# A searched instruction order: weights loaded first on one queue, token LayerNorm moved to GpSimd

## The chip, the cores and the metric

The kernel runs on one core of one Trainium2 chip. The metric is the device time of one execution in microseconds, as the median of several runs. The engines are TensorE (PE; its weight loads are shown apart as PEld), VectorE (DVE), ScalarE (ACT), GpSimd (POOL) and SyncE (SP), which issues transfers. All run side by side, each takes its own instructions strictly in the order in which they were written down, and they wait for one another by semaphores.

## The reference

Two layers; each is an attention block without a softmax over positions, and then a gated block. There are S = 2048 tokens (16 tiles of 128), D = 576 features, H = 32 heads of 18, and F = 4608 hidden features. All inputs are bf16.

```python
def A(x, wqkv, w_phi, wo):
    q, k, v = split(x @ wqkv)                       # 32 heads of 18
    pq, pk = q @ w_phi, k @ w_phi                   # per head
    phi_q = concat(softmax(pq), softmax(-pq))       # over 18 values: 36 features a head
    phi_k = concat(softmax(pk), softmax(-pk))
    kv = einsum("bhsf,bhsd->bhfd", phi_k, v)        # a sum over all tokens
    z  = phi_k.sum(over s)
    o = (phi_q @ kv) / (phi_q @ z + 1e-6)
    return o @ wo

def B(x, w_gate, w_up, w_down):
    return ((x @ w_gate) * (x @ w_up)) @ w_down

x = A_x
for layer in (1, 2):
    x = x + A(layernorm(x), wqkv, w_phi, wo)
    x = x + B(layernorm(x), w_gate, w_up, w_down)
```

`kv` needs every token's `phi_k` and `v` before the first output of the block can be made. So at the start of layer 1 all 16 token tiles go through layer norm, transposition, two projections and the softmax on the key side, and only then the gated block can begin. In the later part of a layer, the key side of the next layer is strewn into the gated block.

## The kernel before

The file does not write its instructions down in order. It describes them as some hundred small threads (generators), and a list scheduler, which runs when the kernel is built, picks the next operation again and again by an estimated time. The recorded order of each engine, with the semaphore waits it needs, is then emitted. Numbers in the code such as `Op(790, ...)` are those estimates in nanoseconds; they steer the order and are no measurements.

The choice of the next operation. `AGES` is a table of biases by thread name which was found by search, `th.age` a bias that a thread sets itself; `alt` offers one operation on several engines and takes the one that would end first:

```python
if r[0] == "alt":
    for i_, (eng, ops) in enumerate(r[1]):
        e_ = self.port_time(eng, ops[0], max(self.free_at[eng], self.ready(th, i_, eng, ops, False), th.t_ready))
        f_ = e_ + sum(o.dur for o in ops) * self.alt_cost[eng]
        if pick is None or f_ < pick[0]:
            pick = (f_, e_, eng, ops)
# ...
key = (est - self.bias.get(int(th.prio), 0.0) - th.age - th.age0 - (self.hold if late else th.boost), -th.prio)
# the smallest key is next
_, th, est = best
if self.fill is not None:
    self.keep_warm(min(pe_est, est))
```

`keep_warm` fills pauses of TensorE with products of a tile of zeros (L935), as many as the estimate says there is room for:

```python
def keep_warm(self, limit):
    t = self.free_at["pe"]
    # ...
    cold = 2.0 if t < 6000.0 else 1.0
    n = int((limit - (150.0 if early else 400.0) - t) / (56.0 * cold))
    for _ in range(n):
        o = self.fill(b, self.pe_mode)     # matmul of zt (128x128 zeros) with itself
        # ... recorded on TensorE if it ends before limit
```

The first loads. `x0` is one token tile (128 x 576, 147 KB), `x` two token tiles, `raw` one of five blocks of the query and key weights (128 x 1216, 311 KB), `wv` the value weights. `sload` is issued by SP, `aload` by ACT after the small `w_phi`:

```python
self.sload = [['x0', 0], ['raw', 0], ['x0', 1], ['raw', 2], ['raw', 3], ['raw', 4], ['wv', 0], ['x', 3]]
self.aload = [['raw', 1], ['x', 1], ['x', 2]]
```

A flag is then computed from the weights: it bounds how large `pq` and `pk` can become. All engines wait for it (L250, L251) and branch: if it is set, the *fast* program follows, in which the exponentials need no subtraction of a maximum; otherwise the *general* one. With these inputs the fast program runs. The flag takes ten products of each of the five weight blocks with themselves (L974), a norm of `w_phi` (L954 to L961), and two last products (L985):

```python
def t_flag(self):
    yield ("age", s.fage2)
    for kt in range(5):
        yield ("wait", ("ld", "raw", s.rord[kt]))
        # ten 128x128 products of Wraw[kt] with itself, into two banks        (L974)
    # two maxima on VectorE, compared with the limit                          (L977, L983)
    # one product with ones, then flag = (sum > 255.5)                        (L985, L987)
    yield ("mark", ("flag",))
    yield ("sig", "branch")
```

Query and key weights are multiplied with `w_phi` on the chip: each block is transposed by TensorE (L1100), evicted (L1103), multiplied with the block diagonal `BDphi` (L1114), and evicted to `Wq` or `Wk` (L1119).

Layer norm of one or two token tiles (`t_ln`). `fast` in this function is not the program but the variant with a TensorE transposition, which only urgent tiles use; the others are transposed by a DMA from `xln`, for which 640 columns are wanted, the last 64 being the last 64 of 576 once more:

```python
# statistics: two bn_stats per tile (L1154), bn_aggr (L1162), -mean (L1168 / L1171)
# rstd = exp(-0.5 * ln(var + eps)) on ScalarE                           (L1175, L1177)
em = [(lambda e, j=j, a=a, b=b, c=c: e.tensor_scalar(xln[:, sl[j], a:b], x_sb[:, ss[j], c:c + b - a],
            s.nmean[:, sl[j]:sl[j] + 1], rstd[:, sl[j]:sl[j] + 1], ALU.add, ALU.mult))
      for a, b, c in ((0, 576, 0), (576, 640, 512))[:2 - fast]]                       # L1187
yield ("alt", [(eng, [Op(d, em[i], ...) for i, d in enumerate(dur)])
               for eng, dur in (("pool", (790, 370)[:2 - fast]), ("dve", (400,) if fast else (400, 215)))[:1 + (fast or boot)]])
```

`boot` is true for the tiles at the start of layer 1. So there each tile's normalisation is one `tensor_scalar` over 576 columns and one over 64, on GpSimd or VectorE.

The key side of a tile: a projection into two banks (L1228, 18 products with 64 rows each, pairs of which share the array), four exponentials on ScalarE (L1349), then

```python
def softmax_tail(self, sm, crit, pz=None, exps=True):
    # sum over 18 values: tensor_reduce 128x1152 on VectorE                   (L1416)
    # 1/sum: reciprocal on VectorE (L1419), or Ln and Exp on ScalarE (L1423, L1427)
    for br in range(2):
        # dd = dd * (1/sum), 128x576, on GpSimd; on VectorE for the last two tiles  (L1431)
```

and 18 products for each pair of tiles that add to `kv` (L1470). The value projection is evicted by ScalarE (L1460). After the last pair: a mask (L1561), the numerator (L1618), a division (L1626 to L1640), the output projection (L1216), layer norm, transposition (L1195, L1198), and the gated block (L1758; downward products L1832 and L1834). Query projections are kept in `xT` and fill TensorE where they can.

Of the kernel before, what the change touches and what calls it, by code (L numbers as in the profile page):

```python
# [8 lines left out]
ALU = mybir.AluOpType  # L9
# [10 lines left out]
    "ain1_0": 96, "ain1_1": 52, "ain1_11": -60, "ain1_12": -492, "ain1_13": 86, "ain1_14": -147, "ain1_5": -137, "ain1_6": -193, "ain1_9": -273,  # L20
    "ain2_14": -438, "ain2_15": -340, "aout1_0": -130, "aout1_1": -102, "aout1_2": -169, "aout1_3": -149, "aout2_0": -365, "aout2_1": 28,
    "aout2_2": -170, "aout2_3": -392, "bar1": -205, "bar2": 31, "bdphi": 104, "bepi0": -915, "bepi6": 256, "bepi7": -330, "flag": -70, "fusek0": -120,
    "fusek1": -40, "fusek2": 301, "fusek3": -147, "fuseq0": -35, "fuseq1": -124, "fuseq2": -148, "fuseq3": -151, "init": 401, "k2_6": -418,
    "k2ln0": 766, "k2ln1": 1415, "kv2_7": -134, "lnA1_0a": 245, "lnA1_0b": 360, "lnA1_2": 62, "lnA1_3": 52, "lnA1_4": -54, "lnB1_0a": -675,
    "lnB1_0b": -631, "lnB2_0a": -815, "lnB2_0b": -579, "pq1_10": -131, "pq1_11": 213, "pq1_2": 262, "pq1_3": -196, "pq1_4": -111, "pq1_5": 12,
    "pq1_6": 145, "pq1_9": 334, "pq2_11": 118, "pq2_12": 428, "pq2_15": 112, "pq2_2": 322, "pq2_3": 281, "pq2_4": 41, "pq2_5": 296, "pq2_6": -35,
    "pq2_8": -91, "v1_0": 39, "v1_1": -420, "v1_11": -111, "v1_13": -244, "v1_15": 580, "v1_2": -281, "v1_3": -122, "v1_5": -127, "v1_6": -124,
    "v1_8": -122, "v2_14": -755, "v2_15": -878,
# [268 lines left out]
class Sched:  # L297

    def __init__(self, tracker):
# [13 lines left out]
        self.fill = None  # L313
        self.pe_switch = 100.0
# [94 lines left out]
    def keep_warm(self, limit):  # L409

        tr = self.tr
        t = self.free_at["pe"]
# [10 lines left out]
        b = max(cand)[1]  # L423
        cold = 2.0 if t < 6000.0 else 1.0
# [10 lines left out]
    def run(self):  # L435
        tr = self.tr
        while True:
# [122 lines left out]
            if r[0] == "ops":  # L560
                eng = r[1]
# [3 lines left out]
                for o in r[2]:  # L565
# [8 lines left out]
                    fin = t + o.dur  # L574
                    tr.record(eng, o.emit, o.reads, o.writes, o.excl, fin, deps)
# [7 lines left out]
            else:  # L583
# [7 lines left out]
                else:  # L591
                    start = max(issue + 1250.0, self.dma_free["sp"])
                    left, u = nbytes, start
                    for end, rate in ((3400.0, 290.0), (5000.0, 150.0), (1e9, 335.0)):
                        if u < end and left > 0:
                            d_ = min(left / rate, end - u)
                            left, u = left - d_ * rate, u + d_
# [3 lines left out]
                fin = max(start + xfer + (self.dma_lat if hasattr(self, "mark_time") else 600.0), issue + 2.1 * sp_time) + (1500.0 if sp_time > 1000 else 0.0)  # L601
# [66 lines left out]
class K:  # L668
    def __init__(self, nc, A_x, A_wqkv, A_w_phi, A_wo, B_w_gate, B_w_up, B_w_down, out, fast, base=None):
# [10 lines left out]
        self.vlead = 5  # L680
        self.row2 = True
        self.wtdma = ''
        self.valt = False
        self.qalt = True
        self.sload = [['x0', 0], ['raw', 0], ['x0', 1], ['raw', 2], ['raw', 3], ['raw', 4], ['wv', 0], ['x', 3]]
        self.aload = [['raw', 1], ['x', 1], ['x', 2]]
        self.rord = (0, 1, 2, 3, 4)
        self.fage = 300
        self.fageq = 0.0
        self.fage2 = 300  # L690
# [4 lines left out]
        self.qlead = 12 if fast else 8  # L695
# [8 lines left out]
        self.pqg = 8 if fast else 10  # L704
# [7 lines left out]
        self.fqp = 6.5 if fast else 6.5  # L712
# [225 lines left out]
    def t_bdphi(self):  # L938
        s = self
        yield ("wait", "init")  # L940
        yield ("wait", ("ld", "wphi5"))
        wb = s.wst5[:].unsqueeze(2).to_broadcast([128, 5, GH, DH])
# [5 lines left out]
    def t_m2(self):  # L948
# [3 lines left out]
        yield ("wait", ("ld", "wphi5"))  # L952
        yield ("age", s.fage2)
# [11 lines left out]
    def t_flag(self):  # L965
        s = self
        yield ("wait", "init")
        yield ("age", s.fage2)
        for kt in range(5):
            yield ("wait", ("ld", "raw", s.rord[kt]))  # L970
# [599 lines left out]
    def t_aout(self, L, st_):  # L1570
# [71 lines left out]
        if st_ >= 2:  # L1642
            ops.append(Op(130, (lambda e: e.tensor_copy(o[:, 576:640], o[:, 512:576])), reads=okeys, writes=okeys))
# [479 lines left out]
```

## Time and profile before

The median of three runs is 1074.42 us (1073.74 to 1075.68). The profiled execution has a span of 1073.7 us and a granted TensorE clock of 0.999.

| engine | busy, us | share | instructions |
|---|---|---|---|
| TensorE products | 1054.6 | 98% | 15797 |
| TensorE weight loads | 808.6 | 75% | 15859 |
| VectorE | 484.3 | 45% | 983 |
| ScalarE | 347.0 | 32% | 839 |
| GpSimd | 196.5 | 18% | 226 |

Points in time that the text comes back to, from the timeline:

| what | us |
|---|---|
| first load issued | 0.79 |
| first product of zeros | 1.03 |
| first product with weights (L974) | 5.45 |
| flag written (L987) | 17.93 to 18.06 |
| first key projection (L1228 with `Wk`) | 20.34 |
| first and last group of key-value products (L1470) | 33.17 and 85.94 |
| first product of layer 1's gated block (L1758) | 102.56 |
| first product of layer 2's gated block | 619.40 |

How to read the lines below. A timeline line has the start, the length, the engine, the line of the kernel, the operation, what it writes and reads, how many there are, and in brackets how long the engine stood idle before it and what ended that. A stage line has a stretch of time and its length, and then for PE, PEld, DVE, ACT and POOL the busy time with the number of instructions in brackets; after them the granted TensorE clock, the mean busy share of the DMA engines, and GB/s. The lengths of single products include their way through the array, and neighbours overlap; so a TensorE that is busy is not one that works at its full pace, and the number of products in a stretch says more. `xln`, `dd` and `ss` are the normalised tokens, the exponentials, and their sums.

### The profile page before, as it was taken

How to read it: one execution, taken by the hardware profiler on the slowest of the kernel's cores; microseconds unless marked ns; L12 is line 12 of the kernel's file. 1: busy time of each engine (PE TensorE's matmuls, PEld its weight loads, DVE VectorE, ACT ScalarE, POOL GpSimd, SP SyncE). 2: the span in 40 equal slices, each digit the busy share in tenths (PEclk: the TensorE clock that was granted, in tenths of full speed). 3: DMA queues.
4: the chain of work that ended last, by engine and by line, in shares of the span. 5: the costliest groups of instructions: out<-in, count | busy, mean ns of one | idle time of the engine just before them, and what ended most of it. 6: DMA issues, size and time to landing. Idle time of an engine off the chain costs nothing.

```text
span 1073.7 us, 34403 instructions
## 1 busy us (share of the span) xinstructions
PE 1054.6 (98%) x15797; PEld 808.6 (75%) x15859; DVE 484.3 (45%) x983; ACT 347.0 (32%) x839; POOL 196.5 (18%) x226
## 2 busy tenths in 40 slices
PE   9989999999999999999999999999999999999997
PEld 6657868778686878878686787777778686868683
DVE  6976526344443635425232754434434243424131
ACT  5777214314241422315141742231313131302030
POOL 2753104022130403103020030201010101000000
PEclk9999999999999999999999999999999999999999
DMA  5395365271826336271605134636271818080604
GB/s 154 95 289 213 47 171 102 69 179 15 226 34 192 69 109 145 33 200 32 204 15 166 35 59 115 144 87 173 61 198 36 223 16 242 17 223 15 210 2 147
DMA packets 177626, 127.79 MB, mean 119 GB/s; under 512 B 96576, under 2 KB 175680, under 8 KB 176320
## 3 DMA queue, kind: packets, MB, share of 16 engines
q1 hardware_dynamic: 176176, 124.57, 44.8%
q8 instruction: 126, 2.06, 0.8%
q10 hardware_dynamic: 1296, 0.92, 0.3%
q14 instruction: 28, 0.23, 0.1%
HBM read 100.82 MB, written 2.36 MB: 96 GB/s over the span
## 4 chain that ended last, share of the span: by engine, by line
PE 94%; DVE 2%; ACT 2%; issue 1%; DMA 0%; SPq 0%
PE ps L1758 53%; PE ps L1832 22%; PE ps L1228 11%; PE ps L1834 4%; PE ps L1618 1%; DVE ss_w4f L1416 1%; DVE xln L1187 1%; PE ps L1470 1%; ACT dd_h1g L1349 1%; PE ps L1216 0%; PE ps L1195 0%; PE ps L974 0%; DMA Wraw<-in_A_wqkv_dram 0%; ACT dd_w3f L1349 0%; PE ps L1114 0%
## 5 line engine op out<-in xcount | busy, mean ns | idle before, releaser
L1758 PE MATMUL ps<-xT,Wg 64*128 64x256 bf16 x4608 | 581.9, 269 | 0.0
L1758 PE MATMUL ps<-xT,Wu 64*128 64x256 bf16 x4608 | 581.1, 269 | 0.0
L1758 PEld LDWEIGHTS ps<-xT,Wg 64*128 64x128 bf16 x4608 | 430.7, 94 | 29.0 <-issue 3.1
L1758 PEld LDWEIGHTS ps<-xT,Wu 64*128 64x128 bf16 x4608 | 431.8, 94 | 27.2
L1807 DVE TENSOR_TENSOR hT<-ps,hT 128x512 bf16<-128x512 f32 x288 | 199.2, 692 | 303.8 <-ACT hT L1805 303.8
L1805 ACT CAST hT<-ps 128x512 bf16<-128x512 f32 x288 | 168.7, 586 | 413.5 <-PE ps L1758 406.5
L1832 PE MATMUL ps<-wdr,hT 128*128 128x512 bf16 x922 | 237.8, 380 | 0.0
L1431 POOL TENSOR_TENSOR dd<-dd,ss 128x576 bf16<-128x576 bf16 x92 | 106.5, 1186 | 488.9 <-ACT ss L1427 488.8
L1834 PE MATMUL ps<-wdr,hT 128*128 128x64 bf16 x960 | 184.9, 193 | 2.3 <-issue 0.5
L1832 PEld LDWEIGHTS ps<-wdr,hT 128*128 128x128 bf16 x960 | 93.9, 98 | 110.9 <-DMA wdr<-in_B_w_down_dram 0.5
L1758 PE MATMUL ps<-xT,Wr 64*128 64x256 bf16 x1152 | 168.2, 269 | 0.0
L1875 DVE TENSOR_TENSOR x_sb<-ps,x_sb 128x64 bf16<-128x64 f32 x32 | 7.1, 220 | 224.3 <-PE ps L1834 224.3
L1187 POOL TENSOR_SCALAR xln<-x_sb,nmean,rstd 128x576 bf16<-128x576 bf16 x86 | 51.9, 610 | 254.4 <-DVE nmean L1168 173.6
L1834 PEld LDWEIGHTS ps<-wdr,hT 128*128 128x128 bf16 x960 | 94.1, 98 | 0.2
L1427 ACT ACTIVATE ss<-ss 128x64 f32<-128x64 f32 x92 | 23.5, 258 | 177.8 <-DVE ss L1416 176.8
L1416 DVE TENSOR_REDUCE ss<-dd 128x64 f32<-128x1152 bf16 x48 | 63.6, 1347 | 20.0 <-ACT dd L1349 18.9
L1758 PEld LDWEIGHTS ps<-xT,Wr 64*128 64x128 bf16 x1152 | 65.1, 94 | 6.2
L1228 PE MATMUL ps<-Wk,xT 64*128 64x288 bf16 x576 | 49.1, 284 | 2.8 <-ACT Wq L1119 1.7
L1228 PE MATMUL ps<-Wv,xT 64*128 64x288 bf16 x576 | 49.8, 283 | 1.6 <-ACT eT L1594 0.5
L1832 PE MATMUL ps<-wdx,hT 128*128 128x512 bf16 x168 | 50.4, 380 | 0.1
L1154 DVE BATCH_NORM_STATS2 st<-x_sb 128x6 f32<-128x288 bf16 x120 | 46.2, 445 | 1.4 <-DMA x_sb<-in_A_x_dram 1.3
L1228 PE MATMUL ps<-Wq,xT 64*128 64x288 bf16 x576 | 41.1, 283 | 0.6 <-ACT dd_w3f L1349 0.4
(128 smaller groups left out, 749.5 us busy)
## 6 DMA issues: line engine op xcount, KB each, us to landing
wdr<-in_B_w_down_dram SPq DMA_DIRECT2D x240, 288.0 KB, 3.6
wdx<-in_B_w_down_dram SPq DMA_DIRECT2D x48, 288.0 KB, 3.7
Wg<-in_B_w_gate_dram SPq DMA_DIRECT2D x4, 1152.0 KB, 13.4
Wu<-in_B_w_up_dram SPq DMA_DIRECT2D x4, 1152.0 KB, 15.6
out_dram<-x_sb SPq DMA_DIRECT2D x16, 144.0 KB, 2.8
x_sb<-in_A_x_dram SPq DMA_DIRECT2D x5, 288.0 KB, 3.3
Wraw<-in_A_wqkv_dram SPq DMA_DIRECT2D x4, 304.0 KB, 5.9
xT<-xln SPq DMA_TRANSPOSE x54, 2.4
```

The costliest lines, as they stand in the source:

```text
L1154: ops.append(Op(d_dve(288), (lambda e, j=j, h=h, src=src: e.bn_stats(st[:, sl[j], 6 * h:6 * h + 6], src)), reads=rd, writes=[("st", sl[j], ...
L1187: em = [(lambda e, j=j, a=a, b=b, c=c: e.tensor_scalar(xln[:, sl[j], a:b], x_sb[:, ss[j], c:c + b - a], s.nmean[:, sl[j]:sl[j] + 1], rstd[ ...
L1228: out.append(Op(61, (lambda e, h=h, k=k, st=(i == 0 and k == 0), sp=(i == 1 and k == 3): e.matmul(s.ps[:, banks[h], 0:N], L[r, k, :], Wm[r ...
L1349: yield ("ops", "act", [Op(d_actc(288), (lambda e, br=br, h=h, bank=bank: e.activation(s.dd[:, sm, 16 * h:16 * h + 16, br, :], s.ps[:, ban ...
L1416: Op(1265, (lambda e: e.tensor_reduce(ss[:, sm, :], e4, AX.X, ALU.add)), reads=s.ddk(sm, 0) + s.ddk(sm, 1), writes=[("ss", sm)]),
L1427: yield ("ops", "act", [Op(200, (lambda e, kw=kw: e.activation(ss[:, sm, :], ss[:, sm, :], **kw)), reads=[("ss", sm)], writes=[("ss", sm)])])
L1431: yield ("alt", [(eng, [Op(dur, (lambda e, ev=ev, rb=rb: e.tensor_tensor(ev, ev, rb, ALU.mult)), reads=s.ddk(sm, br) + [("ss", sm)], write ...
L1758: out.append(Op(54.3, (lambda e, bank=bank, cs=cs, lhsT=lhsT, rhs=rhs, st=st, sp=sp: e.matmul(ps[:, bank, cs].rearrange("p (a n) -> p a n" ...
L1805: yield ("ops", "act", [Op(480, (lambda e, gb=gb, p=p: e.copy(hT[:, p, :], ps[:, gb, :])), reads=[("gu", gb)], writes=[("hT", p)] + (s.raw ...
L1807: yield ("ops", "dve", [Op(600, (lambda e, ub=ub, p=p: e.tensor_tensor(hT[:, p, :], ps[:, ub, :], hT[:, p, :], ALU.mult)), reads=[("gu", u ...
L1832: ops = [Op(d_pe(512), (lambda e: e.matmul(s.ps[:, bank, 0:512], lhsT, s.wslot(slot)[:, fi, 0:512], start=(f == 0), stop=(f == NF - 1))), ...
L1834: Op(d_pe(64) + 3, (lambda e: e.matmul(s.ps[:, z, 64 * sl:64 * sl + 64], lhsT, s.wslot(slot)[:, fi, 512:576], start=(f == 0 and (sl == 0 o ...
```

## The change

1. **Early loads on one queue.** All first loads go through SP; ACT issues only `w_phi`. Weight blocks come first. The flag's products now take the blocks in the order of loading.
2. **Token LayerNorm on GpSimd.** At the start of layer 1, VectorE is no longer offered the normalisation of pairs of tiles (`lndve = False`). The 64 doubled columns are no `tensor_scalar` of their own any more, but one copy for both tiles of a pair, on GpSimd or ScalarE; that holds for all pairs, in both layers.
3. **Zeros in pauses.** The rule of `keep_warm` is the same, but the estimate for the opening is another one: TensorE operations before 6 us are counted at double length, and the pauses come out differently. Within the fast program 23 products of zeros stand where 31 stood.
4. **A mended estimate.** More operations count as holding the port which VectorE and GpSimd share; the early transfer rate and the cost of DMA transpositions that queue are changed.
5. **The search was run again.** `AGES` is replaced as a whole, and with it some steering numbers (`vlead`, `fage`, `fage2`, `qlead`, `pqg`, `fqp`), which say how far one thread may run ahead of another.

All results are computed as before. In the fast program TensorE's instructions are the same but for the zeros; only their places change. Before layer 1's gated block begins there now stand 288 query projection products instead of 252. On VectorE there are 13 fewer normalisations of 576 columns and 11 fewer of 64; on GpSimd 13 more of 576 columns and no more 43 of 64, but 9 copies; ScalarE has 18 such copies.

The diff, cut to its core (`AGES` and repeated hunks left out):

```diff
@@ Sched
+        self.warm_at = 6000.0
-        cold = 2.0 if t < 6000.0 else 1.0
+        cold = 2.0 if t < self.warm_at else 1.0
@@ Sched.run
                     fin = t + o.dur
+                    if eng == "pe" and t < self.warm_at:
+                        fin += o.dur
@@
-                    for end, rate in ((3400.0, 290.0), (5000.0, 150.0), (1e9, 335.0)):
+                    for end, rate in ((3400.0, 290.0), (5000.0, 150.0), (1e9, 350.0)):
@@ K.__init__
-        self.vlead = 5
+        self.vlead = 7
+        self.lndve = False
-        self.sload = [['x0', 0], ['raw', 0], ['x0', 1], ['raw', 2], ['raw', 3], ['raw', 4], ['wv', 0], ['x', 3]]
-        self.aload = [['raw', 1], ['x', 1], ['x', 2]]
-        self.rord = (0, 1, 2, 3, 4)
-        self.fage = 300
+        self.sload = [['raw', 2], ['raw', 1], ['x0', 0], ['raw', 0], ['raw', 3], ['x0', 1], ['x', 1], ['raw', 4], ['x', 2], ['wv', 0], ['x', 3]]
+        self.aload = []
+        self.fage = 150
-        self.fage2 = 300
+        self.fage2 = 600
-        self.qlead = 12 if fast else 8
+        self.qlead = 8 if fast else 8
-        self.pqg = 8 if fast else 10
+        self.pqg = 4 if fast else 10
-        self.fqp = 6.5 if fast else 6.5
+        self.fqp = 6.15 if fast else 6.5
@@ t_bdphi, t_m2
+        yield ("delay", 5000.0)
@@ t_ln
-            em = [(lambda e, j=j, a=a, b=b, c=c: e.tensor_scalar(xln[:, sl[j], a:b], x_sb[:, ss[j], c:c + b - a], s.nmean[:, sl[j]:sl[j] + 1], rstd[:, sl[j]:sl[j] + 1],
-                                                                 ALU.add, ALU.mult)) for a, b, c in ((0, 576, 0), (576, 640, 512))[:2 - fast]]
...
-                           for eng, dur in (("pool", (790, 370)[:2 - fast]), ("dve", (400,) if fast else (400, 215)))[:1 + (fast or boot)]])
+            em = (lambda e, j=j: e.tensor_scalar(xln[:, sl[j], 0:576], x_sb[:, ss[j], :], s.nmean[:, sl[j]:sl[j] + 1], rstd[:, sl[j]:sl[j] + 1], ALU.add, ALU.mult))
...
+                           for eng, dur in (("pool", 790), ("dve", 400))[:1 + (fast or (boot and s.lndve))]])
+        if not fast:
+            xo, xi = xln[:, s0:s1, 576:640], xln[:, s0:s1, 512:576]
+            yield ("alt", [(eng, [Op(dur, em, reads=key("xln"), writes=key("xln"))]) for eng, dur, em in (
+                ("pool", 420, lambda e: e.tensor_copy(xo, xi)), ("act", 210, lambda e: e.copy(xo, xi)))])
@@ softmax_tail
-                                     reads=s.ddk(sm, br) + [("ss", sm)], writes=s.ddk(sm, br))])
+                                     reads=s.ddk(sm, br) + [("ss", sm)], writes=s.ddk(sm, br), port=eng == "dve")])
```

## The prediction

> **What bounds the kernel now.** I read the page first, then the chain that ended last, then a table of stages, then the timeline of the opening, and last the groups of instructions up to 103 us.
>
> ```profile
> PE 1054.6 (98%) x15797; PEld 808.6 (75%) x15859; DVE 484.3 (45%) x983; ACT 347.0 (32%) x839; POOL 196.5 (18%) x226
> PE 94%; DVE 2%; ACT 2%; issue 1%; DMA 0%; SPq 0%
> ```
>
> Tensor work carries 94% of the chain. What other engines can still give is the remaining 6%, some 60 us, and the question is where it lies. The chain from 103 us on shows nearly only tensor lines; the gated blocks cannot be shortened by a new order. From 20 to 80 us the same view names other owners:
>
> ```profile
> by line: PE ps L1228 25.0%; DVE ss_w4f L1416 17.3%; DVE xln L1187 15.3%; ACT dd_h1g L1349 9.3%; ACT dd_w3f L1349 6.2%; ACT ss_w4f L1423 4.2%; issue 3.7%; PE ps L1470 3.4%; DVE st L1154 2.4%; ACT eT L1594 2.1%; ACT xT L1198 2.1%; ACT dd L134
> ```
>
> L1187, the normalisation of tokens on the Vector engine, has 15.3% of 60 us, 9.2 us. The stage table (busy time and instructions of each engine in each stretch) says the same:
>
> ```profile
> 20.00:33.00 13.00, 12.21 (x156) 7.08 (x152) 11.11 (x27) 11.70 (x39) 6.67 (x6) 1.00 0.54 137
> 33.00:53.00 20.00, 19.32 (x301) 14.45 (x299) 19.23 (x39) 14.69 (x54) 13.65 (x14) 1.00 0.25 58
> 53.00:68.00 15.00, 12.47 (x183) 8.25 (x180) 12.48 (x18) 11.84 (x42) 8.91 (x8) 1.00 0.83 165
> 68.00:87.00 19.00, 17.27 (x266) 11.85 (x263) 11.57 (x15) 13.40 (x39) 9.22 (x8) 1.00 1.01 422
> 87.00:102.60 15.60, 15.57 (x214) 10.84 (x210) 11.44 (x27) 12.29 (x31) 2.42 (x2) 1.00 0.52 176
> ```
>
> TensorE looks busy everywhere, but it issues 183 products in 15 us and 266 in 19 us, against 184 in the 10 us from 120 to 130, inside the gated block. A dense run of projections, 128 in 8.03 us, gives 0.0627 us each. At 0.059 us each over this mix, the four stretches to 87 us hold 906 products or 53.5 us of work in 67 us: 13.5 us are stalls. VectorE is full, 19.23 of 20, exactly where the normalisations lie.
>
> **What the skill says.** Four statements bear on this.
> - The Trainium skill, "Perfetto Trace Analysis", section "Identifying the Most-Contended Engine": the busy share of TensorE is no measure of its headroom. The trace agrees: busy 91% from 68 to 87 us with 14.0 products a microsecond, 100% from 120 to 130 with 18.4.
> - "SBUF — State Buffer", section "Who interferes with whom": tensor_scalar on VectorE can enter a mode with two ports, one of them GpSimd's, and whichever comes second is blocked for the whole instruction. The trace agrees:
>
> ```profile
> 20.95 2.12 DVE L1187 TENSOR_SCALAR xln<-x_sb,nmean,rstd 128x576 bf16<-128x576 bf16 x6 [0.34 <-ACT rstd L1177]
> 41.72 3.17 DVE L1187 TENSOR_SCALAR xln<-x_sb,nmean,rstd 128x576 bf16<-128x576 bf16 x4
> 42.46 2.39 POOL L1431 TENSOR_TENSOR dd_w3f<-dd_w3f,ss_w4f 128x576 bf16<-128x576 bf16 x2 [0.78 <-ACT ss_w4f L1423]
> ```
>
> With GpSimd idle six normalising instructions take 2.12 us; with its two products (2.39 us) in between four take 3.17. It recurs at 51.78 and 59.43 us.
> - "GPSIMD Engine Reference", section 8, "Key points": elementwise work is about twice as fast on VectorE. The trace: 820 ns against a median of 423 for the same rows.
> - "TensorE: Matmul & The Clock Gate", Part 1: the array starts at half clock and is released by sustained activity in a free-running window. The trace: ten 128-column products advance 1.07 us at 9.8 and at 11.7 us, and end within 0.72 us at 13.97.
>
> **The change part by part.**
>
> *Opening.* The first weight block (0.311 MB) is issued second now, at 1.24 us, behind a token tile (0.147 MB), shares the engines with a block issued at 1.88 on ACT's queue, and costs the chain 4.17 us (to 5.45). After the change a weight block goes first on SP and nothing large runs beside it. In order, 0.311 MB instead of 0.458 MB at the 253 GB/s of the window 2 to 4 us is 0.6 us, and the issue 0.45 us earlier: about 1.0 us, perhaps 1.7. Agreeing with that, 23 zero products replace 31 (8 x 0.107 = 0.86 us). Ahead of the branch stand no value projections (18 before: 1.45 us from start to end) and one group of token transposes less (0.57 us). So the flag, ready at 18.06 us, should come near 15.5; of those 3 us 2 are only work put behind the branch. Kept: **1.3 us**.
>
> *Normalisation off VectorE.* Before the gated block VectorE has 15 large pieces (9.3 us) and 11 small (5.5) after 18 us. In the new order 4 large remain (4 x 0.42 = 1.7 us): 13.1 us leave. What comes back: 4 more evictions of query weights (4 x 0.42), one of transposed weights (0.48), two reciprocals (2 x 0.55), three transposed token tiles (3 x 0.49), one of eT (0.49): 5.2 us. Net **-7.9 us on VectorE**. GpSimd gets 12 large pieces for one: 11 x 0.82 - 0.4 = +8.6 us. The tail of 64 columns becomes one copy for two tokens' tiles, six of them on ScalarE before the block; estimated at 0.26 us each (like its 64-column activations) 1.6 us, against 6 evictions which it loses.
>
> *What that makes of the pace.* The eight groups of L1470 (each a pair of token tiles) start at 33.2 and end at 86.6 us: about 7.6 us a pair. Demand of a pair after the change, from the mean durations: VectorE 2 x 1.345 (reduce) + 4 x 0.38 (statistics) + 0.33 + about 0.9 (evictions, reciprocal) = 5.5; GpSimd 4 x 1.19 + 2 x 0.82 = 6.4; ScalarE 8 x 0.33 (exponentials) + 4 x 0.36 + 0.7 + 4 x 0.26 + 0.26 + 0.4 = 6.5; TensorE 72 x 0.0627 + 0.8 + about 0.7 for query weights = 6.0. VectorE before: 5.0 + 3.17 = 8.2 where the ports collided. So the bound passes from VectorE at about 8 to three engines near 6.4, and 7 intervals could shorten by (7.6 - 6.5) x 7 = 7.7 us. In-order queues with three engines near full will not get it all; I take three quarters: **5.8 us**.
>
> *Later.* Before, 252 query products precede the gated block; after, 288. These 36 x 0.061 = 2.2 us are only moved, so the block starts 2.2 us less early than the gain. The middle is the same sequence of 144-product downs with projections strewn in: 0. Between the layers the order keeps 28 query products (1.8 us) after the last output projection instead of 54 (3.4 us). In the trace exactly those 3.4 us cover the normalisation (614.36 to 617.77), so a stall of about 1 us may appear: **-0.7**. The ending, 648 gated products and 144 downs, is identical.
>
> Sum: 1.3 + 5.8 - 0.7 = 6.4 us; 1074.4 - 6.4 = 1068.0. The first gated product should then move from 102.6 to 102.6 - 7.1 + 2.2 = 97.7 us.
>
> **Rivals.**
> - *The Vector engine was not the limit, GpSimd becomes it.* For it: GpSimd is already busy 13.65 of 20 us from 33 to 53, and takes twice as long per tile; each tile's products wait behind two normalisations (1.6 us). Against: 6.4 us a pair is still under the present 7.6. It would give 1073 to 1076.
> - *The stalls are chains in order, not load.* From 68 to 87 us no engine but TensorE is above 71%; exponentials (2.42 us in one piece at 72.2) and reduces follow one another. If the new order leaves these waits, only the opening and half of the pace come: 1071.
> - *The new order settles all of it.* Stalls fall from 13.5 to 4 us, the array warms earlier, and the transition costs nothing: 10 to 12 us, 1063. The small number of fillers and the closer order of k, v and q speak for it; that no durations stand behind the order but those of a model speaks against.
>
> **Range and chances.** The three rivals span 1063 to 1075; the pace term has an uncertainty of 4 us, opening and transition 1.5 us each, the run itself 1 us. I give 1061.5 to 1073.5. Over 2% faster needs 21.5 us, more than all stalls before 87 us with the opening together (13.5 + 3): chance 0.01. Over 2% slower needs 21.5 us of new stalls in a sequence that repeats the old in its 900 us of dense work: 0.01. Within 2%: 0.98.
>
> **What would show each step.** Opening: first product on weights near 4.2 us and the flag near 15.5. Normalisation: no piece of several large normalisations on VectorE beside GpSimd products between 25 and 85 us, VectorE's busy time down some 8 us, GpSimd's large pieces near 820 ns. Pace: the eight groups on 6.6 to 6.9 us intervals, the last near 79, GpSimd and ScalarE above 85% between. Transition: a wait of about 1 us before the transposes ahead of layer 2's gated block. It is wrong if the first gated product comes after 102 us, if GpSimd is what the products wait for, or if the dense blocks differ.

## The result, and the profile after

The changed kernel takes 1063.99 us as the median of four runs (1061.64 to 1065.01); the kernel before took 1075.0 us beside it (four runs, 1073.74 to 1075.68). The ratio is 0.9896, 95% interval 0.9876 to 0.9915. That is 11.0 us less, inside the range of 1061.5 to 1073.5 and 4 us below the predicted 1068.0. The profiled execution spans 1062.2 us; the one before spanned 1073.7, so the two traces differ by 11.5 us, and this is the sum to be explained.

The page of the changed kernel, busy time by engine, and the shares of the chain that ended last:

```profile
PE 1051.5 (99%) x15851; PEld 805.1 (76%) x15851; DVE 480.7 (45%) x972; ACT 346.7 (33%) x843; POOL 190.7 (18%) x204
PE 95%; POOL 2%; DVE 1%; ACT 0%; DMA 0%; issue 0%; SPq 0%
```

The share of VectorE has fallen from 2% to 1%, that of ScalarE from 2% to 0%, and GpSimd has come in with 2%. VectorE's busy time over the whole span fell only from 484.3 to 480.7 us. The chain from 20 to 80 us by owner:

```profile
by line: PE ps L1238 37.2%; POOL dd_h1g L1441 19.1%; POOL xln L1194 8.0%; POOL dd_w3f L1441 7.6%; ACT dd_h1g L1359 4.4%; POOL dd L1441 3.9%; PE ps L1480 3.8%; DVE ss_w4f L1426 2.3%; DVE ss L1426 2.0%; PE ps L1205 1.5%; ACT vx_w0g L1470 1.2%
```

Before, L1187 on VectorE (normalisation) held 15.3% and the reduces 17.3% here. Now GpSimd's multiplications (L1441) and normalisations (L1194) hold 38.6%. (The lines of the changed file lie 4 to 12 further down: projections L1238, exponentials L1359, key-value products L1480, gated block L1770.) The stage table, with the columns as before:

```profile
20.00:33.00 13.00, 12.79 (x183) 8.33 (x180) 10.91 (x20) 11.42 (x41) 9.75 (x10) 1.00 0.54 112
33.00:53.00 20.00, 19.78 (x315) 14.55 (x314) 18.24 (x37) 16.84 (x63) 20.00 (x21) 1.00 0.38 75
53.00:68.00 15.00, 14.99 (x249) 11.32 (x245) 9.13 (x9) 12.32 (x43) 13.91 (x13) 1.00 1.02 279
68.00:87.00 19.00, 18.87 (x269) 13.57 (x265) 15.33 (x32) 13.85 (x37) 5.07 (x5) 1.00 1.01 414
87.00:102.60 15.60, 15.60 (x271) 13.06 (x267) 7.75 (x14) 9.30 (x24) 4.66 (x4) 1.00 0.54 89
```

GpSimd is busy 20.00 of 20 us from 33 to 53. That looks like a new bound, and the chain says so as well. But TensorE is busy there for 19.78 us, and from 53 to 68 us it now issues 249 products where it issued 183. The view of what TensorE waited for between 20 and 103 us settles which of the two matters. Before (columns: line, whom it waited for, us in total, times, longest):

```profile
PE ps L1228 <- ACT Wq L1119: 1.7, 1, 1.7
PE ps L1228 <- ACT dd_h1g L1349: 1.1, 2, 0.7
PE ps L1588 <- POOL dd L1431: 0.8, 1, 0.8
PE ps L1228 <- ACT dd_w3f L1349: 0.6, 2, 0.4
PE ps L1228 <- ACT eT L1594: 0.5, 2, 0.3
PE ps L1228 <- ACT dd L1349: 0.3, 1, 0.3
PE ps L1228 <- ACT Wk L1119: 0.2, 1, 0.2
```

and after, the whole answer:

```profile
PE ps L1480 <- POOL dd_h1g L1441: 0.2, 1, 0.2
PE ps L1238 <- ACT dd_h1g L1359: 0.2, 1, 0.2
```

5.2 us of named waits of TensorE's products have become 0.4, and GpSimd, full as it is, kept a product waiting once, for 0.2 us.

Where the 11.5 us lie, from the starts of single products (the first gated product of before stands at 102.39 us; the table ahead of the prediction had 102.56):

| stretch | before | after | difference |
|---|---|---|---|
| start to first key projection | 20.34 | 18.56 | -1.8 |
| to first gated product of layer 1 | 82.05 | 75.11 | -6.9 |
| to first gated product of layer 2 | 517.01 | 513.62 | -3.4 |
| to the end | 454.3 | 454.9 | +0.6 |

In the second stretch stand 36 more query products (2.2 us), so some 9.1 us of stalls went there. The third stretch has 54 fewer (36 that moved ahead and 18 that moved behind; 54 x 0.061 = 3.3 us), the last 18 more: both are work moved, not gained. The first row is the least certain: the key projection of the same order starts up to 3 us earlier or later in other executions (given with the experiments). The eight groups of key-value products start from 33.17 to 85.94 us before (52.77 / 7 = 7.54 us a pair) and from 32.34 to 74.40 after (42.06 / 7 = 6.01).

### The profile page after: what moved, and what is told of

It reads as the page before. It is cut to its first block, busy times and chain, and to the rows that moved or that the text cites. A ratio compares the mean times of both kernels' runs of the same rounds, so it can differ in the third digit from the quotient of the medians.

```text
span 1062.2 us, 34403 instructions
## 1 busy us (share of the span) xinstructions
PE 1051.5 (99%) x15851; PEld 805.1 (76%) x15851; DVE 480.7 (45%) x972; ACT 346.7 (33%) x843; POOL 190.7 (18%) x204
## 4 chain that ended last, share of the span: by engine, by line
PE 95%; POOL 2%; DVE 1%; ACT 0%; DMA 0%; issue 0%; SPq 0%
PE ps L1770 53%; PE ps L1844 23%; PE ps L1238 11%; PE ps L1846 3%; PE ps L1628 1%; POOL dd_h1g L1441 1%; PE ps L1480 1%; PE ps L1226 0%; DMA Wraw<-in_A_wqkv_dram 0%; PE ps L1205 0%; POOL xln L1194 0%; POOL dd_w3f L1441 0%; ACT dd_h1g L1359 0%; POOL dd L1441 0%; PE ps L1121 0%; PE ps L1685 0%
## 5 line engine op out<-in xcount | busy, mean ns | idle before, releaser
L1770 PE MATMUL ps<-xT,Wu 64*128 64x256 bf16 x4608 | 581.6, 270 | 0.0
L1770 PE MATMUL ps<-xT,Wg 64*128 64x256 bf16 x4608 | 581.2, 270 | 0.0
L1770 PEld LDWEIGHTS ps<-xT,Wg 64*128 64x128 bf16 x4608 | 431.4, 94 | 30.4 <-issue 3.3
L1770 PEld LDWEIGHTS ps<-xT,Wu 64*128 64x128 bf16 x4608 | 432.5, 94 | 27.4
L1844 PE MATMUL ps<-wdr,hT 128*128 128x512 bf16 x960 | 244.9, 380 | 0.0
L1441 POOL TENSOR_TENSOR dd<-dd,ss 128x576 bf16<-128x576 bf16 x92 | 106.6, 1184 | 441.7 <-ACT ss L1437 441.7
L1770 PE MATMUL ps<-xT,Wr 64*128 64x256 bf16 x1152 | 165.7, 270 | 0.0
L1194 POOL TENSOR_SCALAR xln<-x_sb,nmean,rstd 128x576 bf16<-128x576 bf16 x56 | 45.4, 821 | 332.4 <-DVE nmean L1175 151.2
L1770 PEld LDWEIGHTS ps<-xT,Wr 64*128 64x128 bf16 x1152 | 63.3, 94 | 6.4
L1844 PE MATMUL ps<-wdx,hT 128*128 128x512 bf16 x192 | 54.3, 380 | 0.1
L1238 PE MATMUL ps<-Wv,xT 64*128 64x288 bf16 x576 | 50.4, 288 | 0.2 <-ACT dd_h1g L1359 0.2
L1238 PE MATMUL ps<-Wk,xT 64*128 64x288 bf16 x576 | 48.5, 283 | 0.0
L1238 PE MATMUL ps<-Wq,xT 64*128 64x288 bf16 x576 | 40.6, 283 | 0.0
```

The lines of the kernel that those rows point to most:

```text
L1194: em = (lambda e, j=j: e.tensor_scalar(xln[:, sl[j], 0:576], x_sb[:, ss[j], :], s.nmean[:, sl[j]:sl[j] + 1], rstd[:, sl[j]:sl[j] + 1], ALU ...
L1238: out.append(Op(61, (lambda e, h=h, k=k, st=(i == 0 and k == 0), sp=(i == 1 and k == 3): e.matmul(s.ps[:, banks[h], 0:N], L[r, k, :], Wm[r ...
L1441: yield ("alt", [(eng, [Op(dur, (lambda e, ev=ev, rb=rb: e.tensor_tensor(ev, ev, rb, ALU.mult)), reads=s.ddk(sm, br) + [("ss", sm)], write ...
L1770: out.append(Op(54.3, (lambda e, bank=bank, cs=cs, lhsT=lhsT, rhs=rhs, st=st, sp=sp: e.matmul(ps[:, bank, cs].rearrange("p (a n) -> p a n" ...
L1844: ops = [Op(d_pe(512), (lambda e: e.matmul(s.ps[:, bank, 0:512], lhsT, s.wslot(slot)[:, fi, 0:512], start=(f == 0), stop=(f == NF - 1))), ...
```

## The experiments

"Order frozen" means that the edit leaves all estimates of the scheduler as they are, so every engine's list stays the same; "built anew" means that the scheduler makes another list. Since the opening differs between executions, two lengths are compared beside the time: from the first key projection to the first gated product (82.05 us before, 75.11 after), and the pace of the groups.

### Old order, longer zeros

Order frozen; nine more zero products behind the 31.

```diff
+        last = (this is zero product number 31)
+            for _ in range(9 * last):
+                e.matmul(s.ps[:, bank, 0:128], s.zt, s.zt)
             return e.matmul(s.ps[:, bank, 0:128], s.zt, s.zt)
```

> The kernel before, order unchanged, with nine more products of zeros behind the 31, so that TensorE works without a break from 1.03 us into the first weight product at 5.45. Theory of the clock (the array of the kernel before stayed at half pace to 12.8 us because its activity broke off from 4.5 to 5.45): ten-product pieces take 0.72 us from about 6 us on, the flag comes near 15 to 16 us instead of 18.06, the time falls by 1.5 to 3 us to about 1072.5. Rival of the loads (only the arrival of the weights counts): flag at 18.0 within 0.3 us, time unchanged at 1075 within 0.7.

Measured: 1074.51 us, ratio 0.9987 (0.9978 to 0.9996), 1.4 us less. The first weight products ran at full pace at once (ten in 0.72 us at 5.13), the flag came at 15.73 instead of 17.93, and the first four groups 2.2 us earlier. That is not shown to be the work of the zeros: two later executions of this order without them (thinned normalisation, delay) had their first weight product at 4.32 us and the flag at 15.24 and 14.93. It was the profile before that was late; it waited 0.93 us for its first weight block. In the trace the 2.2 us were then lost: the fifth group is 0.95 us earlier and the end 0.5 us later. The loss is seen in a table of this kernel in slices of two microseconds; the column behind GpSimd is the granted clock:

```profile
56.00:58.00 2.00, 0.77 (x15) 0.37 (x9) 1.96 (x5) 0.86 (x4) 0.04 (x1) 1.00 1.03 240
58.00:60.00 2.00, 1.10 (x13) 0.55 (x15) 1.96 (x2) 1.95 (x7) 2.00 (x2) 0.89 1.05 225
60.00:62.00 2.00, 2.00 (x18) 1.28 (x20) 1.65 (x2) 0.81 (x4) 1.50 (x2) 0.50 1.22 114
62.00:64.00 2.00, 2.00 (x28) 1.39 (x25) 0.00 (x0) 0.87 (x4) 1.70 (x2) 0.75 0.99 192
```

TensorE stands half idle for four microseconds (the wait of 1.7 us for `Wq` on ScalarE is part of it), and the clock falls to half: 18 products in the slice from 60 to 62, against 36 in a dense slice at the full clock (66 to 68 us of the same trace). In the profile of the kernel before the same pause stands at 58 to 62 us and the clock stayed at 1.00:

```profile
58.00:60.00 2.00, 0.97 (x17) 0.52 (x13) 1.96 (x4) 0.83 (x5) 0.00 (x0) 1.00 0.94 230
60.00:62.00 2.00, 1.08 (x11) 0.53 (x11) 1.96 (x3) 1.95 (x7) 1.84 (x2) 1.00 1.02 230
```

So the old order has a place where the clock may be lost. From the key projection to the gated block this execution needs 83.31 us, 1.26 more than the profile before.

### New order, thin zeros

Order frozen; the zero products have one column instead of 128.

```diff
-        e.matmul(s.ps[:, bank, 0:128], s.zt[0:rows, :], s.zt[0:rows, :])
+        e.matmul(s.ps[:, bank, 0:1], s.zt[0:rows, :], s.zt[0:rows, 0:1])
```

> The changed kernel, order unchanged, its 23 products of zeros cut from 128 columns to one, which keeps them in place but gives TensorE almost no work before the weights come. Theory of the clock: half pace to 8 us or later, flag at 14 to 16 us instead of 12.69, time 1.5 to 3 us longer, about 1066. Rival of the loads: flag at 12.7 within 0.3 us, time 1064 within 1.

Measured: 1067.67 us, ratio 0.9916 (0.9888 to 0.9944). Four of the five flag pieces ran slowly (1.13 to 1.27 us for ten products), the flag came at 14.36 instead of 12.55, and 1.8 us later stands everything up to the gated block (95.44 against 93.67). The stretch from key projection to gated block is 75.2 us, as with full zeros. The other 2 us of the profiled execution are waits for down-projection weights (2.0 us between 96 and 1040 us), which the profile after does not have. That the zeros are worth these 1.8 us is not shown. The execution with shorter normalisations on GpSimd (below) has all its zeros at full width, and the same four slow pieces; its flag came at 14.54. One of the pieces in the changed kernel, here with thin zeros, and there with full ones:

```profile
5.78 0.72 PE L981 MATMUL ps<-Wraw 128*128 128x128 bf16 x10
6.24 1.27 PE L981 MATMUL ps<-Wraw 128*128 128x128 bf16 x10
6.41 1.27 PE L981 MATMUL ps<-Wraw 128*128 128x128 bf16 x10
```

The interval of the ratio also overlaps that of the changed kernel (0.9876 to 0.9915). What the run does show is that in the new order a shift of the opening arrives whole at the gated block.

### Old kernel, only the normalisation moved

Built anew, old biases; pairs of tiles are normalised on GpSimd alone.

```diff
-   ... ("dve", (400,) if fast else (400, 215)))[:1 + (fast or boot)]])
+   ... ("dve", (400,) if fast else (400, 215)))[:1 + fast]])
```

> The kernel before, with the normalisation of pairs of token tiles at the start of layer 1 on GpSimd alone (two pieces a tile as before, 576 and 64 columns); loads, biases and all else old, so the opening is the same. Theory of the port (VectorE blocked by GpSimd set the pace): groups of L1470 about 6.6 to 7.0 us apart instead of 7.6, first gated product near 98 us instead of 102.6, time 1069 to 1071. Rival of the search (the pace came from the new order, and GpSimd with 2.4 us more a pair is no gain without it): 7.4 us or more a pair, time 1073 to 1078.

Measured: 1073.52 us, ratio 0.9987 (0.9975 to 0.9999), 1.4 us less with an interval that hardly excludes none. From key projection to gated block it needs 80.95 us instead of 82.05. Its stage from 33 to 53 us:

```profile
33.00:53.00 20.00, 17.02 (x261) 12.25 (x259) 14.00 (x28) 14.80 (x50) 19.41 (x23) 1.00 0.31 71
```

VectorE fell from 19.23 to 14.00 us, GpSimd rose from 13.65 to 19.41, and TensorE issues fewer products than before (261 against 301). The groups stand 7.67 us apart. In this order GpSimd is waited for (1.1, 1.0 and 0.4 us, once each). The move alone mostly passes the load on.

### New kernel, VectorE offered the normalisation again

Built anew with the new biases.

```diff
-        self.lndve = False
+        self.lndve = True
```

> The changed kernel with VectorE offered again for the normalisation of pairs of tiles at the start of layer 1. Theory of the port: pieces of normalisation on VectorE are stretched again where GpSimd works, groups about 6.8 to 7.2 us apart instead of 6.1, time 1068 to 1071. Rival of the search: the list estimate, which now knows the port for more operations, places them without loss; time 1064 within 1.5.

Measured: 1070.34 us, ratio 0.9946 (0.9930 to 0.9962), 6 us longer than the changed kernel. The groups stand 7.23 us apart. VectorE took seven large pieces before the gated block, and where they met GpSimd the port shows again (three of them took 1.29, 0.59 and 1.28 us):

```profile
51.23 1.69 DVE L1194 TENSOR_SCALAR xln<-x_sb,nmean,rstd 128x576 bf16<-128x576 bf16 x2
```

Two pieces take 1.69 us, beside 0.42 us for a single one of this size in the kernel before, where GpSimd does not work beside it. The seven take 4.8 us in all, while the seven intervals between the groups grew by 7 x (7.23 - 6.01) = 8.5 us. So a part may be their own time; that the rest is an order which was not searched for these pieces is an inference, not shown.

### Old order, VectorE's normalisation shortened

Order frozen; the large pieces for pairs of tiles that stand on VectorE at the start of layer 1 write 64 of 576 columns. The rest of those tiles is left out. A piece gets shorter by less than its columns (0.42 to 0.30 us where GpSimd is idle):

```profile
18.82 0.30 DVE L1189 TENSOR_SCALAR xln<-x_sb,nmean,rstd 128x64 bf16<-128x64 bf16 x1
```

The eleven of them fall from 7.6 to 3.2 us together. The small pieces stay, three of them still stretched to 1.09 us. So 4.4 us leave VectorE, of the 13.1 us that the change takes from it.

```diff
+            th_ = [tensor_scalar(xln[:, sl[j], 0:64], x_sb[:, ss[j], 0:64], ...)] + em[1:] if boot else em
-   Op(d, em[i], ...)
+   Op(d, (th_ if eng == "dve" else em)[i], ...)
```

> The kernel before with its order frozen; the normalisations of pairs that stand on VectorE at the start of layer 1 write 64 of their 576 columns (the rest of the tile is left out). Theory VectorE (the pace of 7.6 us a pair was set by VectorE's load and the port): the groups of key-value products come on intervals of about 6.6 us, the first gated product moves from 102.6 to 96-98, the time falls by 4 to 7 us. Rival chains (the order itself holds the pace; exponentials, reduces and multiplications follow one another wherever VectorE's time goes): intervals stay at 7.3 us or more, the first gated product at 100.5-102.6, the time falls by 0 to 2 us.

Measured: 1071.08 us, ratio 0.9930 (0.9909 to 0.9951). The time and the first gated product (97.33) are as the theory VectorE has them, but the opening of this execution was early too (key projection at 17.64). Without it: from key projection to gated block 79.7 us instead of 82.05, and the groups stand 7.20 us apart instead of 7.54, where 6.6 was expected. So these 4.4 us of VectorE's time and the port were worth 2.4 us in this stretch, and 3.6 against the longer zeros, whose clock fell in it. The time fell by more: 7.5 us by the ratio (5.3 to 9.8), 5.1 by the median of the 24 executions of the kernel before that ran beside it (1076.22). A part of this is clock (a mean of 0.998 against 0.997); the rest is not explained. All this is a lower bound of what VectorE's load was worth, since most of the 13.1 us stayed. Waits of other owners were left: exponentials in `dd_w3f` still hold 2.42 us in one piece, and a multiplication on GpSimd is still waited for 0.8 us.

### New order, GpSimd's normalisation shortened

The same for the pieces on GpSimd in the changed kernel, order frozen; the rest of those tiles is left out. Twelve pieces get shorter by half (0.82 to 0.40 us), 5.0 us together.

```diff
+            th_ = tensor_scalar(xln[:, sl[j], 0:64], x_sb[:, ss[j], 0:64], ...) if boot else em
-   Op(dur, em, ...)
+   Op(dur, th_ if eng == "pool" else em, ...)
```

> The changed kernel with its order frozen; the normalisations of pairs on GpSimd at the start of layer 1 write 64 of their 576 columns. GpSimd is busy 20.0 of 20 us from 33 to 53 us there, TensorE 19.8 with 315 products. Theory TensorE (the new order has reached TensorE's own pace, GpSimd is full but nothing waits for it): the groups keep their 6.1 us, the first gated product stays within 0.7 us of 93.7, the time falls by 0 to 0.7 us. Rival GpSimd (it has become the bound): the first gated product comes 2 to 5 us earlier and the time falls by as much.

Measured: 1066.66 us, ratio 0.9887 (0.9854 to 0.9920). Nothing is gained. The flag came late in the profiled execution (14.54, with four slow flag pieces), the key projection at 20.45 and the gated block at 95.58: 75.1 us, as in the changed kernel, groups 6.00 us apart. Its stage from 33 to 53 us:

```profile
33.00:53.00 20.00, 20.00 (x328) 15.06 (x324) 18.36 (x39) 15.97 (x60) 17.65 (x20) 1.00 0.56 94
```

GpSimd has 2.35 us of room now and TensorE runs no faster behind it. The full GpSimd of the profile after is not a bound: shorter by 5.0 us, it brings none of the 2 to 5 us that this rival expected.

### New kernel, old biases

Built anew; only the table of biases is that of the kernel before.

```diff
-AGES = {...new...}
+AGES = {...old...}
```

> The changed kernel with the table of biases of the kernel before; everything else as changed, the schedule built anew. Theory content (the moved normalisation, the loads and the steering numbers bring the gain, the table refines it): 1065 to 1068 us. Rival search (the gain lies in an order found for exactly these pieces; another table loses the fit): 1069 to 1075 us, TensorE with pauses again between 33 and 87 us.

Measured: 1075.96 us, ratio 0.9996 (0.9985 to 1.0006). The whole gain is gone, although the loads, the zeros, the normalisation on GpSimd and the steering numbers are the new ones and the flag comes at 13.35. The chain from 20 to 80 us has a transfer as its longest piece (start, length, what):

```profile
58.80 8.99 DMA xT<-xln
```

and the stage table of the same kernel shows the stretch around it:

```profile
53.00:68.00 15.00, 12.60 (x180) 8.09 (x177) 6.79 (x8) 10.65 (x34) 11.34 (x11) 1.00 0.80 141
```

A transposition by DMA stands on the chain for 8.99 us, and TensorE issues 180 products in the stretch where the changed kernel issues 249.

### The loads alone, both ways

The changed kernel with the old loads (and without the delay in `t_bdphi`), and the kernel before with the new ones; both built anew.

```diff
# in the changed kernel; the reverse in the kernel before
-        self.sload = [['raw', 2], ['raw', 1], ['x0', 0], ...]
-        self.aload = []
+        self.sload = [['x0', 0], ['raw', 0], ['x0', 1], ['raw', 2], ...]
+        self.aload = [['raw', 1], ['x', 1], ['x', 2]]
```

> The changed kernel with the loads of the kernel before (two queues, token tile first, weight blocks in their old order, the delay ahead of the block diagonals' products removed), the schedule built anew with the new table. Theory opening (the earlier flag is passed on): the flag comes at 16 to 18 us, the first gated product 3 to 5 us later than 93.7, the time 1067 to 1069 us. Rival slack (what the opening gives is given back before the gated block, as in the order of before): at most 1.5 us longer, 1064 to 1065.5 us.

> The kernel before with the loads of the changed one (one queue, weight blocks first, the flag's products in the order of loading), all else as before, the schedule built anew. Theory fit (a rebuilt order without a search for it loses as much as it gains): flag 2 to 3 us earlier, the time 1073 to 1080 us. Rival opening (the loads bring their own gain in any order): 1071 to 1072.5 us.

Measured: the changed kernel with old loads 1088.06 us, ratio 1.0093 (1.0067 to 1.0119); the kernel before with new loads 1076.88 us, ratio 1.0024 (1.0008 to 1.0040). The first is 24 us longer than the changed kernel, far outside both expectations, and not for a late flag: it stands at about 12.8 us, where 16 to 18 was expected. Between the second and third group lie 21.5 us (34.82 to 56.30), in which the lists wait for each other. The second has its first weight product at 3.66 instead of 5.45 us (4.32 in later executions with the old loads), its flag at 16.8, and still ends no earlier. So the early flag does not come with the loads: the old loads with the new biases have it at 12.8, the new loads with the old biases at 16.8. Neither time says what the loads are worth; both fit the reading that an order built without a search for exactly these operations loses more than the operations bring.

### A delay behind the flag, both ways

Order frozen; TensorE's first instruction of the fast program is written 41 times. The other engines start as before.

```diff
+                if engname == "pe":
+                    ops[0] = (waits, (lambda e: [emit(e) for _ in range(41)][-1]), me)
```

> The kernel before with its order frozen; TensorE's first product of the fast program is repeated 40 times, so TensorE starts some 2.3 us later behind the flag while the other engines start as before. Theory slack (the old order has TensorE pauses of its own before the gated block, which take up a shift of TensorE's start): the first gated product comes at most 1.2 us later than in an undelayed execution with the same flag, the time rises by 0 to 1.2 us. Rival (a delay passes through whole): the time rises by 2.0 to 2.6 us.

> The changed kernel with its order frozen and the same 40 repeats behind the flag. Theory TensorE (from the flag on nothing but TensorE's own pace is left, so a delay passes through whole, and so did the earlier flag): the groups of key-value products, the first gated product of both layers and the end all come 2.0 to 2.6 us later. Rival slack: less than 1.2 us reaches the gated block.

Measured: the repeats took 2.2 us in both. Old order: 1076.81 us, ratio 1.0014 (1.0002 to 1.0027), 1.5 us more and between the two expectations, with an interval of 0.2 to 2.9 us that touches both. Its trace is compared with that of the longer zeros, which has the same order: key projection and first group 1.42 us later, fourth group only 0.47, fifth 0.68, gated block 0.67. So about half passes through. The clock fell in the same pause once more, as the slices of the delayed old order show:

```profile
58.00:60.00 2.00, 1.00 (x11) 0.53 (x11) 1.93 (x4) 1.92 (x8) 1.57 (x2) 1.00 0.76 157
60.00:62.00 2.00, 1.63 (x16) 1.01 (x16) 2.00 (x2) 0.99 (x4) 1.97 (x2) 0.62 1.04 221
62.00:64.00 2.00, 2.00 (x22) 1.24 (x20) 0.12 (x1) 0.51 (x2) 1.23 (x2) 0.53 1.25 156
```

New order: 1067.3 us, ratio 0.9920 (0.9896 to 0.9944), 3.3 us above the changed kernel. Key projection 1.62 us later than in the profile after (whose own opening lost 1.2 us, see below), first group 1.64, gated block 2.78 (a wait of 0.9 us for a transposition by DMA came in at 64 us), layer 2's gated block 2.64, the end 3.3. The execution with the longer zeros (next), which kept its clock too, is the better measure: its flag stood 0.62 us earlier, 2.2 us come from the repeats, and the key projection and the first four groups are 2.9 us later than there. Nothing of the delay is taken up before the gated block.

### New order, longer zeros

Order frozen; nine more zero products behind the first 23.

```diff
+        last = (this is zero product number 23)
+            for _ in range(9 * last):
+                e.matmul(s.ps[:, bank, 0:128], s.zt, s.zt)
             return e.matmul(s.ps[:, bank, 0:128], s.zt, s.zt)
```

> The changed kernel, order frozen, with nine more products of zeros behind the first 23, so that TensorE works without a pause up to about 4.3 us. Theory clock (the half pace of the flag's products still costs 1 to 2 us in many executions, longer zeros release the clock more surely): 1062 to 1063.5 us and a narrower spread. Rival (the zeros now stand in front of the first weight block and only cost their own time): 1064 to 1065 us.

Measured: 1064.11 us, ratio 0.9895 (0.9871 to 0.9918), the same as the changed kernel; the spread (1062.59 to 1065.74) is no narrower. The zeros moved the first weight product from 3.68 to 4.43 us. The trace shows something else, which the profile after had hidden. TensorE stands idle before and behind the flag, and in the profile after the clock fell behind it (slices of the changed kernel):

```profile
12.00:14.00 2.00, 0.72 (x11) 0.52 (x11) 1.29 (x5) 0.41 (x2) 0.78 (x4) 1.00 0.02 8
14.00:16.00 2.00, 2.00 (x23) 1.06 (x19) 1.97 (x7) 0.98 (x2) 0.32 (x2) 0.67 0.75 228
16.00:18.00 2.00, 2.00 (x18) 1.25 (x18) 1.10 (x5) 1.29 (x4) 0.00 (x0) 0.50 0.19 67
```

With the longer zeros the same pause passed without a loss (slices of this experiment):

```profile
14.00:16.00 2.00, 2.00 (x29) 1.32 (x28) 2.00 (x7) 1.23 (x4) 0.62 (x3) 1.00 0.64 174
16.00:18.00 2.00, 2.00 (x35) 1.57 (x35) 1.97 (x9) 1.81 (x6) 0.00 (x0) 1.00 0.34 121
```

There the key projection starts at 17.33 us instead of 18.56 and the gated block at 92.41 instead of 93.67, again 75.1 us apart. The end is the same all the same: layer 2's gated block is 0.6 us earlier, with 0.8 us of waits for down-projection weights, and the rest is lost after it. One execution cannot tell whether the longer zeros or chance kept the clock; the delayed new order kept it without them. None of the versions tried beats the changed kernel.

## Why the prediction was right, and where its steps failed

**The result lies in the range, 4 us below the predicted time.** The sum 1.3 + 5.8 - 0.7 was mis-sized in the second term and wrong in the third; the first cannot be judged from the traces.

**Opening, 1.3 us: not decided, and its reason failed.** Predicted were a first weight product near 4.2 us (measured 3.68) and a flag near 15.5 (measured 12.55). I had read one execution's opening as the kernel's. The 4.17 us of its first weight block were not usual: in the delayed and the thinned execution of the same order the first weight product stood at 4.32 instead of 5.45, so the new loads bring it forward by 0.6 us, not by 1.8. The flag of the old order stood at 14.9 to 17.9 us, that of the new one at 12.5 to 14.5 with full zeros; and it is early with the new biases even under the old loads (12.8). At the key projection little of that is left, as the step "only work put behind the branch" says: the old order reaches it at 20.34, 18.14 and 17.64 us, the new one at 18.56, 17.33 and 20.45 (the delayed ones left out). The executions differ more than the orders, so the -1.8 us in the table of stretches can come from which two were profiled.

**Pace, 5.8 of 7.7 us: mis-sized; 9.1 measured.** The step that failed is "the bound passes from VectorE at about 8 to three engines near 6.4". (The 7.6 us before ran from the first start to the last end; from start to start it is 7.54.) The pace became 6.01 us a pair, which is the fourth number of that same list, TensorE's 6.0. TensorE is dense there, a delay of TensorE goes through it whole, and shortening GpSimd's pieces by half changed nothing. The measured pace is below the 6.4 and 6.5 counted for GpSimd and ScalarE, so these were no bounds. I had read a load per pair as a steady pace; but GpSimd is full only up to 53 us and has room later (13.91 of 15 us, then 5.07 of 19), so its work seems to run ahead of the groups that use it. "In-order queues with three engines near full will not get it all" is what the search got round. The mechanism I put ahead, VectorE's load and its port, is real: 4.4 us less on VectorE gave 2.4 to 3.6 us of the stretch in the old order. Its share of the 9.1 is not settled, because the other 8.7 us of normalisation stayed on VectorE in that run. It does not work without an order that fits: moved by itself the normalisation gives nothing in pace (7.67 us a pair) and 1.4 us in time, and with everything else new but the biases nothing in time either. So the order found for these pieces is needed for the gain, and none of the parts that were tried alone holds it. Whether a new search over the old pieces would have found as much was not tried and stays open.

**Transition, -0.7: wrong.** No stall appeared. The stretch before layer 2's gated block is closed up in the profile after:

```profile
603.77 1.89 PE L1238 MATMUL ps<-Wq,xT 64*128 64x288 bf16 x28
605.59 1.08 PE L1205 MATMUL ps<-ident,xln 128*128 128x128 bf16 x12
606.61 0.67 PE L1238 MATMUL ps<-Wq,xT 64*128 64x288 bf16 x8
607.29 0.28 PE L1770 MATMUL ps<-xT,Wg 64*128 64x256 bf16 x1
```

28 query products of 1.9 us were enough to cover the normalisation, and eight more cover the way from the transposes to the block. I had taken the 3.4 us of products that stood there before for the time that the normalisation needs.

**"Later: 0" and the moved 2.2 us: right.** 36 products moved ahead of the block and 18 behind it explain the -3.4 us. The 18 are worth an estimated 1.1 us behind it, where +0.6 was measured.

**The rivals.** "GpSimd becomes the bound" has the profile's look for it, and is refuted by the shortened pieces. "Chains in order" has the old list for it, in which waits stay when VectorE's pieces get shorter, and the list built anew with the old biases. "The new order settles all of it, 10 to 12 us, 1063" is what came out, except that its earlier warm array is no steady part of it. I had held against it that only a model's durations stand behind the order; that deserved less weight, since a search needs the model only to rank orders.

**What would have shown it wrong.** The first gated product came at 93.67, not after 102; the dense blocks are alike. VectorE's busy time fell by 3.6 us in all, not 8: between key projection and gated block it is 65.28 against 58.09, 7.2 us, and 3.6 us more are spent elsewhere.

## What to carry to other kernels

When an engine other than the bound shows 20 of 20 us busy, look at who waits for it before calling it the limit: here it cost 0.2 us, and taking a part of its work away gave nothing. In a kernel of strictly ordered queues, a change of place (another engine, another load order) is worth what a new order makes of it; a change taken alone or undone alone measures the lost fit rather than the change, so freeze the order and thin one cost instead, and count how much of the cost the thinning took: shortening to 64 of 576 columns left 3.2 of 7.6 us. One profile of an opening is not the kernel's opening: under one order the flag came up to 3 us apart. An opening gain is worth its full size only when the bound engine has no pauses left behind it.

## What was not expected of the hardware

TensorE lost its clock after pauses much shorter than I would have thought harmful. The Trainium skill, "TensorE: Matmul & The Clock Gate", section "HAM oscillation — how this bites in real kernels", warns of idle gaps over some 3.4 us. Here the longest single wait was 1.7 us, in four microseconds of which TensorE worked about half (0.77 + 1.10 and 1.24 + 1.00 us), and the clock fell to half for 3.4 us in two of the three profiled executions of the old order that have this pause; the third had 0.97 + 1.08 us of work and kept it. Around the flag 0.72 us of work in 2 us, with a longest wait of 0.98 us, came before such a fall in the profile after. It came in three of the five profiled executions of the new order (from 14.68, 17.02 and 17.19 us on), and not in those with the longer zeros and with the delay. So pauses below the gap of that section can come before a loss of clock here, and whether they do changes from one execution to the next.

That is also a good part of the spread. In 102 executions of the kernel before (one of 1219 us left out) the time falls by 0.86 us for each 0.001 that the mean granted clock rises (correlation -0.67); by calculation from the span, half pace for 2.1 us lowers the mean by 0.001 and costs 1.07 us.
